# Attention and feed-forward kernel: inputs in tile order, row stacks by SBUF copies in place of DMA transposes

## The chip, the cores and the metric

The kernel runs on one core of one Trainium2 chip. The metric is the device time of one execution in microseconds; a lower time is better. Runs are repeated on the chip, and the median of the runs is quoted.

## The reference

Three layers follow one another; all of it is float32.

1. Causal attention with decay, 4 batches, 8 heads, 576 tokens, head dimension 64: `scores = q k^T / 8 + cum_t - cum_s`, where `cum` is the cumulative sum of `log(clip(f, 1e-4, 1))` per head; entries above the diagonal are masked; softmax over s; then times v.
2. A gated feed-forward layer with spatial mixing, on x of 4 x 576 x 512: `h = relu(x w_in)`; u and v are its two halves of 512 columns; v is normalised over its columns; `v_s[t] = sum_s w_spatial[t, s] v_n[s] + b_spatial[t]`; output `(u * v_s) w_out`.
3. A channel-mixing layer: `xk` and `xr` mix each token with the token before by `mu_k` and `mu_r`; `k = relu(xk w_k)`; output `sigmoid(xr w_r) * (k^2 w_v)`.

## The kernel before, in words

**Precision.** Products need more precision than one 16-bit pass gives. q and k are scaled by a power of two and split into a high and a low half-precision part. For each score tile two matmuls are added (L302): 128 rows that hold `k high` over `k low` against `q low` over `q high` (tiles kT and qT), and 67 rows that hold `k high` against `q high` with three rows for the cumulative sums (tiles kA and qA). The transposed scores (L335) are the same with 69 rows: the two further rows of qA carry the row maxima, high and low part.

**Work by pairs of heads.** A pair p is two heads, 16 pairs in all. `load` (L208 to L216) brings k and q of a pair with tokens on partitions, in rows of 64 values, into one of three buffers `knat`/`qnat`, by three DMAs each. `qksq` (L66) sums squares on ScalarE, `qkscale` (L78 to L250) makes the power of two on VectorE after a matmul with ones (L71), `qkhi` (L260 on ScalarE for k, L262 on VectorE for q) writes the high parts and `qklo` (L270 on VectorE) the low parts into `nk` or `nq`, side by side; a DMA transpose of 128 x 1280 half-precision values (L272) turns them into kT or qT. `kaux` (L278, L279) and `qaux` (L284) copy one half of kT and qT into kA and qA and load the rows of sums from the DRAM tile `cumd`; `crow` (L288, GpSimd) writes the constant rows of qA. Then come the scores (L302), the row maxima (L311, VectorE), and `mrow`: the maxima are split (L318, L319), turned by a matmul (L321), copied out (L323), written to the DRAM tile `md` (L325) and read back into two rows of qA (L326). `scoreT` (L335, then the exponential, L339), the causal mask (L344, GpSimd), the product with v (L357), the copy out of PSUM (L365), and per pair the reciprocals of the row sums, which go through DRAM (`head`, `recip`: L368, L375, L378, L381), and the normalisation (L388, GpSimd).

**v** is loaded per batch in five blocks of 128 tokens, two DMAs each (L222); between the two heads of a pair stand 64 columns of ones, which a memset writes once (L178), so that the product with v gives row sums too.

**The feed-forward layer** runs between the attention work of later pairs: `w_in` is loaded and converted from eight blocks at the start (L90, L97, L100 to L105, L440, L441), v half (L504), normalisation (L512 to L547), u half (L558, L560), spatial mixing (L575, L578) with the transposed weights `wspT`. `weights_spatial` (L444 to L485) loads w_spatial by rows, splits it block by block into high and low part, adds the bias in three half-precision columns (L473, L477), and transposes each block by DMA (L483).

**The last part** (L715) multiplies with w_out, w_k, w_r and w_v in single precision; its weights are converted on ScalarE and VectorE from about 395 us on, after the pool of the attention tiles is released; `mu` is loaded first there (L660).

**Order.** `plan_attention` and `plan_mlp` give each step a due time in units of one head and a priority (table `P`); `run` calls the steps in that order. The framework then orders each engine's instructions by its own model of time, except those that `pin` keeps in program order. Almost all DMAs are issued by SyncE (SP), whose queue runs in order: a DMA that waits holds up what is queued behind it. At the start ScalarE issues the first loads of q, f and one block of w_in.

## Time and profile before

| what | value |
|---|---|
| runs (3) | 752.95 to 754.21 us, median 753.43 us |
| profiled execution: span from first to last instruction | 750.9 us |
| profiled execution: its own time | the page gives none beyond the span; the runs shown lie 2.0 to 3.3 us above it |
| granted TensorE clock, mean | 0.970 |
| busy: PE, VectorE, ScalarE, GpSimd | 674.9, 426.8, 372.2, 184.5 us |
| DMA packets, bytes | 130681, 69.78 MB |

How to read the profile: PE is TensorE's matmuls and PEld its weight loads, which overlap them; DVE is VectorE, ACT ScalarE, POOL GpSimd, SP SyncE, and SPq, ACTq the queues of DMA issues of an engine. L272 is line 272 of the kernel. Busy time leaves out register, branch and semaphore instructions and DMA issues. A DMA share of 1 means that all 16 DMA engines are busy. `m<-xx,moe_w_k` means: tile m is written from tiles xx and moe_w_k. In brackets stands how long the engine was idle before an instruction, and what released it.

### The profile page before, as it was taken

Reading aid. Unit: us, or ns where it says so; the run is one execution under the profiler, and the core shown is the slowest. Engines: PE = TensorE matmul, PEld = TensorE weight load, DVE = VectorE, ACT = ScalarE, POOL = GpSimd, SP = SyncE. Lnnn points to the kernel's source line nnn. Section 1 sums busy time; section 2 is a strip of 40 time slices with the busy share of each in tenths; the row PEclk is TensorE's granted clock in tenths of the full one; section 3 lists DMA queues with packets and bytes.
Section 4 is the critical chain, followed back from the end, with each engine's and each line's share of the span. In section 5 each row is a group of like instructions: output and inputs, shape, how many; then the busy total and the mean of one; then the engine's idle time right before and its main releaser. Section 6 shows DMA issues by size and latency. Waiting matters only on the chain.

```text
span 750.9 us, 11016 instructions
## 1 busy us (share of the span) xinstructions
PE 674.9 (90%) x3718; PEld 499.5 (67%) x3718; DVE 426.8 (57%) x1147; ACT 372.2 (50%) x740; POOL 184.5 (25%) x385
## 2 busy tenths in 40 slices
PE   0377878989998999999997679999999999999997
PEld 0245545647775677666774458788888888888886
DVE  5987786666655656646026879988225512632342
ACT  4626786666426854355505539747225412622431
POOL 7122645555324544445321201000000000000000
PEclk9998968999999999999999899999999999999999
DMA  9997666765655234410025453450100100010010
GB/s 228 203 204 158 168 138 131 147 137 107 126 133 122 56 71 99 97 27 18 18 64 184 146 192 124 140 164 15 42 27 16 57 0 15 1 56 1 1 57 28
DMA packets 130681, 69.78 MB, mean 93 GB/s; under 512 B 114704, under 2 KB 115312, under 8 KB 130624
## 3 DMA queue, kind: packets, MB, share of 16 engines
q1 hardware_dynamic: 128032, 67.89, 37.1%
q10 hardware_dynamic: 2592, 1.19, 0.7%
q8 instruction: 29, 0.48, 0.3%
q14 instruction: 28, 0.23, 0.1%
HBM read 42.06 MB, written 9.79 MB: 69 GB/s over the span
## 4 chain that ended last, share of the span: by engine, by line
PE 60%; DMA 16%; DVE 10%; POOL 5%; issue 3%; ACT 3%; SPq 1%; DVEq 0%; ACTq 0%; POOLq 0%
PE m L715 40%; PE o L357 7%; DMA sr<-rd 3%; POOL x L388 3%; PE m L575 3%; PE m1v L504 3%; PE s L302 3%; PE t L335 2%; PE m1u L558 2%; DMA rd<-r 2%; DVE junk L311 2%; DMA r<-rd 2%; DMA wst<-in_moe_w_k_dram 1%; DMA rd<-xo 1%; DMA wst<-in_moe_w_in_dram 1%
## 5 line engine op out<-in xcount | busy, mean ns | idle before, releaser
L357 PE MATMUL o<-e,v 128*128 128x320 f32 (+4 forms) x448 | 114.0, 384 | 5.5 <-POOL e L344 3.7
L715 PE MATMUL m<-xx,moe_w_k 128*128 128x512 f32 (+1 forms) x480 | 107.5, 373 | 0.4 <-ACT x L710 0.4
L715 PE MATMUL m<-moe_w_v,k 128*128 128x512 f32 x432 | 104.8, 391 | 0.0
L339 ACT ACTIVATE e<-t,qa 128x512 f32<-128x512 f32 (+1 forms) x128 | 72.6, 590 | 50.4 <-PE t L335 50.1
L311 DVE CUSTOM_DVE_ANT_0 junk<-s,mask 128x512 bf16<-128x512 f32 (+4 forms) x160 | 75.9, 474 | 37.8 <-PE s L302 32.2
L715 PEld LDWEIGHTS m<-xx,moe_w_k 128*128 128x128 f32 x480 | 84.0, 188 | 18.1 <-ACT x L710 0.9
L357 PEld LDWEIGHTS o<-e,v 128*128 128x128 f32 x448 | 78.5, 199 | 23.7 <-POOL e L344 6.1
L715 PEld LDWEIGHTS m<-moe_w_v,k 128*128 128x128 f32 x432 | 80.7, 188 | 17.7
L344 POOL TENSOR_SCALAR_AFFINE_SELECT e<-e 128x128 f32<-128x128 f32 (+1 forms) x160 | 52.2, 342 | 125.5 <-ACT e L339 123.0
L751 DVE TENSOR_TENSOR tmp<-tmp 128x512 f32<-128x512 f32 (+1 forms) x40 | 25.5, 638 | 88.1 <-ACT tmp L750 87.9
L302 PE MATMUL s<-kT,qT 128*128 128x512 f16 (+2 forms) x192 | 55.8, 299 | 21.6 <-DVE nm L311 13.7
L504 PE MATMUL m1v<-win,xt 128*128 128x512 f16 x240 | 61.5, 397 | 0.0
L388 POOL TENSOR_TENSOR x<-xo,sr 64x576 f32<-64x576 f32 x32 | 47.0, 1469 | 47.6 <-DMA sr<-rd 46.4
L715 PE MATMUL m<-gh,moe_w_out 128*128 128x512 f32 (+1 forms) x240 | 55.1, 380 | 3.5 <-DVE u L578 3.5
L335 PE MATMUL t<-qA,kA 69*128 69x512 f16 (+2 forms) x192 | 51.6, 294 | 7.3 <-DMA qA<-md 6.7
L558 PE MATMUL m1u<-xt,win 128*128 128x288 f16 x384 | 53.6, 286 | 4.5 <-ACT u L560 4.5
L750 ACT ACTIVATE tmp<-m 128x512 f32<-128x512 f32 (+1 forms) x40 | 22.1, 556 | 71.6 <-PE m L715 71.4
L575 PE MATMUL m<-wspT,vn 128*128 128x288 f16 x384 | 54.4, 290 | 3.0 <-DVE u L578 2.3
L302 PE MATMUL s<-kA,qA 67*128 67x512 f16 (+2 forms) x192 | 50.6, 300 | 4.0 <-DMA kA<-kT 3.7
L701 POOL COPY x<-x 128x4 f32<-128x4 f32 x4 | 3.5, 884 | 198.1 <-ACT x L710 198.1
L715 PEld LDWEIGHTS m<-gh,moe_w_out 128*128 128x128 f32 x240 | 43.3, 193 | 13.0 <-DVE u L578 3.8
L335 PE MATMUL t<-qT,kT 128*128 128x512 f16 (+2 forms) x192 | 51.4, 293 | 0.0
(159 smaller groups left out, 1083.8 us busy)
## 6 DMA issues: line engine op xcount, KB each, us to landing
sr<-rd SPq DMA_DIRECT2D x32, 144.0 KB
gd<-u SPq DMA_DIRECT2D x16, 288.0 KB
out_dram<-o SPq DMA_DIRECT2D x18, 256.0 KB
knat<-in_k_dram SPq DMA_DIRECT2D x32, 128.0 KB
v<-in_v_dram SPq DMA_DIRECT2D x32, 128.0 KB
g<-gd SPq DMA_DIRECT2D x16, 256.0 KB
wst<-in_moe_w_k_dram SPq DMA_DIRECT2D x8, 512.0 KB
wst<-in_moe_w_v_dram SPq DMA_DIRECT2D x8, 512.0 KB
```

Source lines behind the costliest of these rows:

```text
L302: self.nc.tensor.matmul(s[:, o:o + n], self.tok(qn, p, h, 128 * ib - 64, 128)[0:r], self.tok(kn, p, h, k0, n)[0:r], start=(j == 0), stop=( ...
L311: self.nc.vector.tensor_tensor_reduce(out=self.junk[r0:, 0:n], in0=self.s[u % 2][r0:, o:o + n], in1=self.mask[r0:, m0:m0 + n], op0=ALU.add ...
L335: self.nc.tensor.matmul(t[:, o:o + n], self.tok(kn, p, h, 128 * c, 128)[0:r], self.tok(qn, p, h, q0, n)[0:r], start=(j == 0), stop=(j == 1))
L339: self.nc.scalar.activation(self.e[g][:, 512 * u:512 * u + n], t[:, 0:n], AF.Exp, scale=self.qa[p][:, 5:6])
L344: self.nc.gpsimd.affine_select(out=e, in_=e, pattern=[[1, n]], compare_op=ALU.is_ge, fill=0.0, base=0, channel_multiplier=-1)
L357: self.nc.tensor.matmul(o[:, 256 + f:256 + q1], v[:, c, h // 2, 64 * (h % 2):64 * (h % 2) + 128], e[:, off:off + q1 - f], start=(c == 0), ...
L388: self.nc.gpsimd.tensor_tensor(self.xp[r], self.xo[h][r], self.sr[r], ALU.mult)
L504: nc.tensor.matmul(self.m1p, xt[:, xs, 128 * j:128 * j + 128], self.win[:, ws, kc, 512:1024], start=(kc == 0 and n == 0), stop=(kc == 3 an ...
L558: self.nc.tensor.matmul(o, self.win[:, ws, kc, fs], self.xt[(4 * b + kc) % 8][:, xs, ts_], start=(kc == 0 and n == 0), stop=(kc == 3 and n ...
L575: nc.tensor.matmul(o, pairs[n][0], pairs[n][1], start=(n == 0), stop=(n == 13))
L715: self.nc.tensor.matmul(out, l, r, start=(first and j == 0), stop=(last and j == len(pairs) - 1))
L751: nc.vector.tensor_tensor(tmp[:, 0:n], tmp[:, 0:n], tmp[:, 0:n], ALU.mult)
```

## The change

The host hands q and k over as [16 pairs, 128, 576], two heads of 64 dimensions on the partitions and tokens along the row; v in blocks of 128 tokens with the ones and the zeros already between and behind the heads; w_spatial transposed, with its last 64 rows repeated; b_spatial as one row; mu in rows of four. In the kernel, one DMA loads k or q of a pair into one of two buffers `kraw`/`qraw`, the high and low parts are tiles of 128 x 576 of their own (two buffers each), and `stack` copies, for each head and each of k and q, three blocks of 64 rows by DMA from SBUF to SBUF: two into kT or qT and one into kA or qA. For the first pair the copies of q are issued by ScalarE. The loads are due 0.1 later. The rows of maxima go from SBUF into qA directly. The spatial weights are split in place into `wspT` without a transpose; the bias is split in one row of 576, held on three partitions, and its three parts are copied by DMA into three rows of `wspT`. `init` clears the columns of each tile that no stack writes.

```diff
-        self.nat = {(nm, i): at.tile([128, 2, 5, 64], F32, name=f"{nm}nat{i}") for nm in "kq" for i in range(3)}
+        self.raw = {(nm, i): at.tile([128, S], F32, name=f"{nm}raw{i}") for nm in "kq" for i in range(2)}
...
     def load(self, p, nm, q=None):
-        q = q or self.nc.sync
-        b, h0 = p // 4, 2 * (p % 4)
-        t, src = self.nat[nm, p % 3], self.a[nm]
-        for h in range(2):
-            q.dma_start(t[:, h, 1:5], src[b, h0 + h, 64:self.S].rearrange("(c p) d -> p c d", p=128))
-        q.dma_start(t[64:128, :, 0], src[b, h0:h0 + 2, 0:64].rearrange("h p d -> p h d"))
+        (q or self.nc.sync).dma_start(self.raw[nm, p % 2], self.a[nm][p])
 
     def vload(self, b, c):
-        t, src = self.v[b % 2], self.a["v"][b]
-        t0, tn = KB[c]
-        for e in range(2):
-            self.nc.sync.dma_start(t[:tn, c, :, 128 * e:128 * e + 64], src[e::2, t0:t0 + tn].rearrange("h p d -> p h d"))
+        self.nc.sync.dma_start(self.v[b % 2][:, c].rearrange("p a d -> p (a d)"), self.a["v"][b, :, c])
...
     def qkhi(self, p, nm, eng):
-        src = self.nat[nm, p % 3].rearrange("p h c d -> p (h c) d")
-        t = self.n16["n" + nm].rearrange("p h c d -> p (h c) d")
-        s = self.qa[p][:, 2 + n:3 + n]
-        hi = t[:, :, 64 * n:64 * n + 64]
+        hi = self.hi[nm] = self.at.tile([128, self.S], F16, tag="hi" + nm, bufs=2, name="hi" + nm)
+        src, s = self.raw[nm, p % 2], self.qa[p][:, 2 + n:3 + n]
...
     def qklo(self, p, nm):
-        nc.vector.scalar_tensor_tensor(t[:, :, 64 - 64 * n:128 - 64 * n], src, s, t[:, :, 64 * n:64 * n + 64], ALU.mult, ALU.subtract)
-        T = self.T[nm + "T", p % 3]
-        nc.sync.dma_start_transpose(out=T[:, 0:10], in_=t.rearrange("p c d -> p (c d)"))
+        hi = self.hi[nm]
+        lo = self.lo[nm] = self.at.tile([128, self.S], F16, tag="lo" + nm, bufs=2, name="lo" + nm)
+        nc.vector.scalar_tensor_tensor(lo, self.raw[nm, p % 2], self.qa[p][:, 2 + n:3 + n], hi, ALU.mult, ALU.subtract)
+
+    def row(self, nm, p, r0, r1, h):
+        return self.T[nm, p % 3].rearrange("p c t -> p (c t)")[r0:r1, 640 * h + 64:640 * h + 64 + self.S]
+
+    def stack(self, p, nm, h, q=None):
+        q = q or self.nc.sync
+        hi, lo = self.hi[nm][64 * h:64 * h + 64], self.lo[nm][64 * h:64 * h + 64]
+        up, down = (hi, lo) if nm == "k" else (lo, hi)
+        q.dma_start(self.row(nm + "T", p, 0, 64, h), up)
+        q.dma_start(self.row(nm + "T", p, 64, 128, h), down)
+        q.dma_start(self.row(nm + "A", p, 0, 64, h), hi)
 
     def kaux(self, p):
-        nc.sync.dma_start(t[0:64, 0:10], self.T["kT", p % 3][0:64, 0:10])
...
-    def qaux(self, p):
-        nc.sync.dma_start(self.T["qA", p % 3][0:64], self.T["qT", p % 3][64:128])
...
     def mrow(self, p):
-        d = self.hl.tile([2, 1280], F16, tag="md", bufs=2, name="md")
-        nc.sync.dma_start(d.rearrange("i (c t) -> (i c) t", t=128), r)
-        nc.sync.dma_start(self.T["qA", p % 3][67:69].rearrange("p c t -> p (c t)"), d)
+        for i in range(2):
+            nc.sync.dma_start(self.T["qA", p % 3][67 + i:68 + i], r[10 * i:10 * i + 10])
...
     def weights_spatial(self):
+        nc.sync.dma_start(ws, a["moe_w_spatial"].rearrange("c p t -> p c t"))
+        nc.sync.dma_start(wb, a["moe_b_spatial"].to_broadcast([3, S]))
...
-            for i in range(3):
-                x = nc.vector.tensor_copy(nf[:tn, 128 + i:129 + i], wbt)
...
-            self.pin(nc.scalar.mul(nf[:tn, 256:768], src[:, 0:512], s))
-            nc.scalar.mul(nf[:tn, 0:64], src[:, 512:S], s)
-            nc.scalar.mul(nf[:tn, 64:128], src[:, 512:S], s)
-            nc.vector.scalar_tensor_tensor(nf[:tn, 192:256], src[:, 512:S], s, nf[:tn, 0:64], ALU.mult, ALU.subtract)
-            nc.vector.scalar_tensor_tensor(nf[:tn, 768:1280], src[:, 0:512], s, nf[:tn, 256:768], ALU.mult, ALU.subtract)
-            nc.sync.dma_start_transpose(out=self.wspT[:, :, t0:t0 + tn], in_=nf[:tn])
+        pb = stp.tile([3, 3, S], F16, name="pb")
+        for i in range(3):
+            if i == 0:
+                self.pin(nc.vector.tensor_scalar(wb, wb, sw[0:3, 1:2], None, op0=ALU.mult))
+            nc.vector.tensor_copy(pb[:, i], wb)
+            if i < 2:
+                nc.vector.tensor_tensor(wb, wb, pb[:, i], ALU.subtract)
+        for i in range(3):
+            nc.sync.dma_start(self.wspT[i:i + 1, 1], pb[i:i + 1, i])
...
+            self.pin(nc.scalar.mul(hi, ws[:, c], s))
+            self.pin(nc.vector.scalar_tensor_tensor(lo, ws[r, c], s[r], hi[r], ALU.mult, ALU.subtract))
...
     def plan_attention(self):
-            add(T + P["aux"], 2, self.kaux, p)
-            add(T + P["aux"] + 0.1, 2, self.qaux, p)
+            for h in range(2):
+                add(T + P["aux"] + 0.2 * h, 2, self.stack, p, "k", h)
+                add(T + P["aux"] + 0.2 * h, 2, self.stack, p, "q", h, nc.scalar if p == 0 else None)
+            add(T + P["aux"], 3, self.kaux, p)
```

## Rows read from the trace of the kernel before

**Rows 1.** The page, parts 1 and 2: busy time of PE; DMA packets.
```profile
PE 674.9 (90%) x3718; PEld 499.5 (67%) x3718; DVE 426.8 (57%) x1147; ACT 372.2 (50%) x740; POOL 184.5 (25%) x385
...
DMA packets 130681, 69.78 MB, mean 93 GB/s; under 512 B 114704, under 2 KB 115312, under 8 KB 130624
```

**Rows 2.** Windows by stage; columns as the header line of the answer names them.
```profile
core 0: us, PE busy (x) PEld busy (x) DVE busy (x) ACT busy (x) POOL busy (x), PEclk, DMA share, GB/s
0.00:60.00 60.00, 26.36 (x122) 15.59 (x122) 47.37 (x139) 30.03 (x63) 24.59 (x63) 1.00 0.97 209
60.00:130.00 70.00, 57.19 (x297) 37.29 (x297) 51.63 (x200) 48.31 (x108) 31.25 (x57) 0.80 0.70 150
130.00:400.00 270.00, 260.66 (x1731) 178.34 (x1730) 140.59 (x469) 134.96 (x278) 117.27 (x238) 0.99 0.41 90
390.00:400.00 10.00, 10.00 (x68) 6.35 (x66) 3.54 (x10) 1.94 (x3) 2.04 (x2) 1.00 0.57 173
400.00:450.00 50.00, 34.04 (x221) 24.51 (x220) 38.76 (x73) 27.35 (x55) 7.90 (x25) 0.90 0.50 163
450.00:750.90 300.90, 296.66 (x1354) 243.75 (x1352) 148.49 (x269) 131.54 (x240) 3.54 (x4) 1.00 0.14 47
```

**Rows 3.** Timeline of the start, all engines: start us, duration us, engine, line.
```profile
9.14 0.72 ACT L66 ACTIVATE junka<-knat 128x640 bf16<-128x640 f32 x1
...
17.62 0.87 DVE L270 SCALAR_TENSOR_TENSOR nk<-knat,qa,nk 128x640 f16<-128x640 f32 x1
...
21.39 0.62 SPq L90 DMA_DIRECT2D wst<-in_moe_w_in_dram  x1
...
23.36 0.96 PE L302 MATMUL s<-kT,qT 128*128 128x512 f16 x2 [7.90 <-DMA kT<-nk]
...
28.01 0.96 PE L302 MATMUL s<-kA,qA 67*128 67x512 f16 x2 [3.69 <-DMA kA<-kT]
...
28.78 0.68 DVE L311 CUSTOM_DVE_ANT_0 junk<-s,mask 128x512 bf16<-128x512 f32 x1
```

**Rows 4.** Waits of PE: total us, times, longest.
```profile
PE s L302 <- DVE nm L311: 13.7, 16, 3.3
...
PE t L335 <- DMA qA<-md: 6.7, 5, 2.5
```

**Rows 5.** Timeline at 311 to 319 us: SP's queue and PE.
```profile
312.91 1.28 SPq L325 DMA_DIRECT2D md<-mr  x1
...
314.24 1.35 SPq L272 DMA_TRANSPOSE qT<-nq  x1
...
316.33 0.22 SPq L326 DMA_DIRECT2D qA<-md  x1
...
316.65 0.35 SPq L580 DMA_DIRECT2D gd<-u  x1
...
317.89 0.39 PE L335 MATMUL t<-qA,kA 69*128 69x512 f16 x1 [1.46 <-DMA qA<-md]
```

**Rows 6.** Issues of SP by tile (knat, then kT): ns min/median/max.
```profile
L215 SPq DMA_DIRECT2D knat<-in_k_dram x32: 368/504/1272, 0.8 to 235.7; - x32
...
L272 SPq DMA_TRANSPOSE kT<-nk x16: 1267/1393/1837, 19.7 to 311.5; - x16
L278 SPq DMA_DIRECT2D kA<-kT x16: 487/520/599, 23.4 to 317.1; - x16
```

**Rows 7.** The chain that ended last: start us, us, what.
```profile
115.63 3.67 DMA wspT<-n
...
318.73 1.83 DMA rd<-xo
```

**Rows 8.** Groups of instructions by line and shape, VectorE.
```profile
L270 DVE SCALAR_TENSOR_TENSOR nq<-qnat,qa,nq 128x640 f16<-128x640 f32 x16 | 16.3, 1016 | 0.1
...
L270 DVE SCALAR_TENSOR_TENSOR nk<-knat,qa,nk 128x640 f16<-128x640 f32 x16 | 14.8, 926 | 4.3 <-ACT nk L260 4.2
...
L262 DVE TENSOR_SCALAR nq<-qnat,qa 128x640 f16<-128x640 f32 x16 | 9.9, 622 | 1.0 <-DMA qT<-nq 0.9
```

More of the change, by code (lines that the diff above doesn't have):

```diff
@@ L141, in setup @@
         self.junka = at.tile([128, 640], BF16, name="junka")
-        self.n16 = {x: at.tile([128, 2, 5, 128], F16, name=x) for x in ("nk", "nq")}
         self.T = {(nm, i): at.tile([128, 11 if nm[0] == "k" else 10, 128], F16, name=f"{nm}{i}") for i in range(3) for nm in ("kT", "kA", "qT", "qA")}
@@ L163, in setup @@
         self.vp, self.vv, self.s = {}, {}, {}
+        self.hi, self.lo = {}, {}
     def init(self, i):
@@ L168, in init @@
         if i < 3:
-            for nm in ("kT", "kA"):
-                g.memset(self.T[nm, i][:, 10], 0.0)
-            t = self.T["kA", i].rearrange("p c t -> p (c t)")
-            g.memset(t[64:69, 0:1280], MS)
-            for h in range(2):
-                g.memset(t[64:69, 640 * h:640 * h + 64], 0.0)
-        elif i < 5:
-            t = self.v[i - 3]
-            x = g.memset(t[:, :, :, 64:128], 1.0)
-            if i == 4:
-                self.pin(x)
-            g.memset(t[64:128, 4], 0.0)
-        elif i == 5:
-            for nm in "kq":
-                g.memset(self.nat[nm, 2][0:64, :, 0, :], 0.0)
-        else:
+            g.memset(self.T["kA", i].rearrange("p c t -> p (c t)")[64:69, 0:1280], MS)
+            for nm in ("kA", "kT", "qT", "qA"):
+                t = self.T[nm, i]
+                if nm[0] == "k":
+                    g.memset(t[:, 10], 0.0)
+                g.memset(t[:, 0:10:5, 0:64], 0.0)
+        elif i > 5:
             self.pin(g.memset(self.xt[i - 6][:, :, 576:640], 0.0))
@@ L448, in weights_spatial @@
         ws = stp.tile([128, 5, S], F32, name="ws")
-        wb = stp.tile([128, 5, 1], F32, name="wb")
-        nc.gpsimd.memset(ws[64:128, 4, :], 0.0)
-        nc.gpsimd.memset(wb, 0.0)
-        nc.sync.dma_start(ws[:, 0:4], a["moe_w_spatial"][0:512].rearrange("(c p) s -> p c s", p=128))
-        nc.sync.dma_start(ws[0:64, 4], a["moe_w_spatial"][512:S])
-        nc.sync.dma_start(wb[:, 0:4], a["moe_b_spatial"][0:512].rearrange("(c p o) -> p c o", p=128, o=1))
-        nc.sync.dma_start(wb[0:64, 4], a["moe_b_spatial"][512:S, None])
+        wb = stp.tile([3, S], F32, name="wb")
+        nc.gpsimd.memset(am, 0.0)
+        nc.gpsimd.memset(self.wspT[0:64, 1], 0.0)
+        nc.sync.dma_start(ws, a["moe_w_spatial"].rearrange("c p t -> p c t"))
+        nc.sync.dma_start(wb, a["moe_b_spatial"].to_broadcast([3, S]))
         yield
@@ L611, in plan_attention @@
     def plan_attention(self):
-        add, G = self.add, self.B * self.H
+        nc, add, G = self.nc, self.add, self.B * self.H
         for p in range(G // 2):
@@ L857, with laid @@
     from concourse.bass_utils import run_bass_kernel_spmd as _run
+    def laid(name, x):
+        if name in "qk":
+            return x.transpose(0, 1, 3, 2).reshape(16, 128, 576)
+        if name == "v":
+            p = _np.zeros((4, 640, 4, 192), x.dtype)
+            p[:, 0:576, :, 64:128] = 1.0
+            p[:, 0:576, :, 0:64] = x[:, 0::2].transpose(0, 2, 1, 3)
+            p[:, 0:576, :, 128:192] = x[:, 1::2].transpose(0, 2, 1, 3)
+            return p.reshape(4, 5, 128, 768).transpose(0, 2, 1, 3)
+        if name == "moe_w_spatial":
+            t = x.T
+            return _np.concatenate([t, t[512:576]]).reshape(5, 128, 576)
+        if name == "moe_b_spatial":
+            return x[None]
+        if name in ("moe2_mu_k", "moe2_mu_r"):
+            return x.reshape(4, 128).T
+        return x
     nc = _bacc.Bacc("TRN2", target_bir_lowering=False, num_devices=1)
@@ L861 @@
     for name in _INS:
-        arr = _np.ascontiguousarray(inputs[name])
+        arr = _np.ascontiguousarray(laid(name, inputs[name]))
         if arr.dtype == _np.float64:
```

34 lines of the change are left out of this document (12 added, 22 removed).

## The prediction

> **What bounds the kernel now.** I read the page first, then the windows by stage, then the timeline of the start, then the waits of PE and the queue of SP. The page gives PE 674.9 us of a span of 750.9 us [rows 1], so 76 us are left in which PE has no matmul, and nothing in the change alters the number of PE's instructions in its long stages. What can be won is idle time and granted clock. The windows say where both lie [rows 2]: to 60 us PE is busy 26.4 of 60 us, from 60 to 130 us 57.2 of 70 us at a clock of 0.80, from 130 to 400 us 260.7 of 270 us, from 400 to 450 us 34.0 of 50 us, and after 450 us it is full. The share of DMA is 0.97 to 60 us, 0.70 to 130 us and 0.14 at the end. The change works in the first three stages; the last is bound by PE and only moves forward with its start.
>
> In the start [rows 3] the reader is to see two chains that meet. ACT sums the squares of the first k from 9.14 us. The last low part of the first pair ends at 18.49 us, its transposes are issued then, the first score matmul runs at 23.36 us, and its second half, which needs the copy into kA, at 28.01 us. Beside it, SP gets to the fourth block of the feed-forward weights only behind both transposes (21.39 us); VectorE converts that block before it takes the first row maximum at 28.78 us. VectorE is busy 47.4 of the first 60 us [rows 2] although the first k lands only at about 9 us: after that it is close to being the bound of the start itself.
>
> Later the waits of PE tell the rest [rows 4]: 13.7 us for row maxima, 6.7 us for the rows of maxima that reach qA by way of the DRAM tile md. At 312 us one sees how the second comes about [rows 5]: SP issues the write of md (1.28 us), a transpose (1.35 us), and only at 316.33 us the read of md into qA; PE then stood 1.46 us.
>
> **The change, part by part.**
>
> *Loads of q, k, v.* Per pair six issues become two, per batch ten for v become five. An issue for k takes 0.50 us (two of them) or, from the line of the first 64 tokens, about the same [rows 6], so some 3 us of SP per pair become 1 us. Packets under 512 B are 114704 of 130681 now [rows 1]; those of q, k and v, 256 B long, go. What that is worth: the DMA engines move 209 GB/s at a share of 0.97 in the first 60 us and 173 at 0.57, or 304 GB/s at a full share, where long weight rows are moved [rows 2]. The first k and q are 0.59 MB, at 304 GB/s 1.9 us; with 0.5 us for the issue [rows 6], the 1.8 us of a transfer of 2.2 KB (rd from xo, [rows 7]) and some waiting behind one another they land at about 5 us instead of 9 us. v now carries its zeros and ones, 1.97 MB per batch instead of 1.18 MB: the rest of DMA's time hides it (share 0.41 from 130 to 400 us), and without that cover it would cost 0.79 MB / 304 GB/s = 2.6 us per batch.
>
> *Transposes become stacks.* Per pair two transposes (1.4 us of SP each) and two copies (0.52 us each) go, 3.8 us [rows 6]; twelve copies of 64 rows come. No row shows such a copy; the nearest is the copy of 64 rows into kA, 0.52 us, and the lower bound is the 0.35 us of an issue with 128 long rows [rows 5]. Twelve are 4.2 to 6.2 us; I take 6 us. With the loads SP has per pair 3.0 + 3.8 = 6.8 us before and 1.0 + 6.0 = 7.0 us after. SP is not relieved, but its pieces are smaller. At the start half of the twelve go on ACT's queue: 3 us of issuing on an engine that is busy 30 of the first 60 us [rows 2], behind which only weight conversions and sums of squares wait.
>
> What the start gains: the bound above is the whole stretch from the last low part to the first full score, 28.01 - 18.49 = 9.5 us; below it is nothing, if VectorE's work decides and does not begin earlier. From the first landing to the first row maximum VectorE takes 28.8 - 9 = 19.8 us, nearly all of it work; begun 4 us earlier it is done at about 24.8 us. **I take 4.0 us** (0 to 9.5).
>
> *The detour through md.* From the issue of its write to that of its read SP shows 3.4 us at 312.91 us [rows 5]; the straight copies need no second wait. Of PE's 6.7 us **I take 5.0 us** (0 to 6.7); the row copies still queue behind others.
>
> *Shapes.* 640 columns become 576. The low parts take 1016 and 926 ns, the high part on VectorE 622 ns [rows 8]: a tenth of 2564 ns is 0.26 us per pair. ACT wins as little. VectorE limits PE in the first four pairs alone, so **1.0 us** (0 to 16 x 0.26 = 4.2).
>
> *Spatial weights.* Their five transposes go (one stands on the chain with 3.67 us, [rows 7]), with them two small ACT copies per block. On VectorE 25 operations on a single column become six on 576 columns of three rows, about 0.6 us each by the 622 ns above, so 3.6 us that are not surely less than what goes. **I take 1.0 us** (-1, if VectorE has more to do, to the 3.7 us of the chain).
>
> *mu.* Two loads of single words become loads of rows. They land before 400 us, where PE is busy 10.00 of 10 us [rows 2], so **nothing**; if that cover were gone, some of the 16 us in which PE idles from 400 to 450 us could come or go. Memsets that go or come on GpSimd: nothing, since GpSimd is busy 24.6 of the first 60 us and the conversions of the start do not pass through it.
>
> Sum: 4.0 + 5.0 + 1.0 + 1.0 = 11 us; 750.9 - 11 = 739.9 us of span. The three runs shown are 752.95 to 754.21 us, 2 to 3 us above the profiled span; with 2.5 us the forecast is **742.4 us**, 1.5% below the median.
>
> **Rivals.**
>
> *A, the start is VectorE's and the rest was hidden:* only some 4 us of waits go, 749 us. For it: VectorE at 47.4 of 60 us. Against it: its first work waits for a landing.
>
> *B, slower:* the twelve copies stand in SP's queue in one block between a pair's recip chain and its rows of maxima. The plan puts stacks and reciprocals at the same moment of the pair. Today a delay of 3.4 us on SP in front of the rows left PE idle for 1.46 us [rows 5]; a block of 6 us would leave it idle 2 to 2.5 us more, in 15 later pairs at 2 us some 30 us, less the 11 us won: 772 us. It decides when the block ends later than about 2 us after the cast of the maxima. Against it: the stacks are due 1.2 heads before their scores, some 12 us, so they can stand elsewhere. The Trainium skill (DMA: Bandwidth & Descriptors, Anatomy of one DMA) gives a transfer a fixed cost of about 2 us that is mostly the wait for completion; by that rule twelve transfers issued one behind the other pay it once, and B is weaker. The short transfer above agrees on the size, and no row here shows the overlap of twelve.
>
> *C, more:* the stage from 60 to 130 us has 12.8 us idle and a clock of 0.80 [rows 2]. If the stalls that go are those before which the clock fell, up to a fifth of 57.2 us, 11.4 us, is won too: 731 us. The Trainium skill (TensorE: Matmul & The Clock Gate, Part 1) says that an idle PE is set back to half clock, so that a stall costs more than its length; the windows from 60 to 130 us agree in kind.
>
> *D, no change:* the time saved comes back at 400 to 450 us, where ACT and VectorE convert weights, 752.5 us.
>
> **Chances.** Forecast (736 to 748 us) 0.52; C 0.20 and still lower 0.03; A 0.08; D 0.06; B 0.11. Range: the upper bounds are 9.5 + 6.7 + 4.2 + 3.7 = 24.1 us, 729 us, and half of C's clock below that, some 724 us; the high end is D with a little of B, 754 us. A measurement of this kernel tells 0.2% (1.5 us) from no change. Faster 0.83 (forecast, C, lower, A), same 0.06, slower 0.11.
>
> **What would show it.** Right: first full score near 22 us and first row maximum near 25 us; no wait of PE for md; a share of DMA clearly under 0.97 to 60 us; few packets under 512 B. Wrong: PE waiting for stacks or rows of maxima (B); first row maximum still at 28 us (A); PE idle for over 20 us from 400 to 450 us (D).

## The result, and the profile after

The changed kernel takes 760.81 us (760.02 to 761.82, 4 runs); the kernel before, on the same chip, 753.19 us (752.14 to 754.21, 4 runs). The ratio is 1.0107, with a 95% interval of 1.0083 to 1.0131: **slower by 1.1%**, where 1.5% faster was forecast. The profiled execution took 761.82 us with a span of 760.1 us, 9.2 us more than before.

The page and the waits of TensorE in the changed kernel, to be laid beside [rows 1] and [rows 4]; the columns of the waits are total us, times, longest:

```profile
PE 673.4 (89%) x3718; PEld 499.3 (66%) x3718; DVE 419.1 (55%) x1122; ACT 368.4 (48%) x730; POOL 178.2 (23%) x376
...
DMA packets 44464, 69.95 MB, mean 92 GB/s; under 512 B 11556, under 2 KB 24452, under 8 KB 44407
```
```profile
PE tot L71 <- ACT junka L66: 19.0, 2, 12.9
...
PE tot L71 <- ACT win L66: 7.3, 1, 7.3
PE o L339 <- POOL e L326: 6.8, 7, 2.7
...
PE t L317 <- DMA qA<-mr: 2.9, 3, 1.5
```

Everything that the change does directly is there. Short packets fell from 114704 to 11556; VectorE, ScalarE and GpSimd have less to do (419.1, 368.4 and 178.2 us against 426.8, 372.2 and 184.5); the wait for the rows of maxima fell from 6.7 to 2.9 us. And TensorE, with 1.5 us less to do, stands idle longer. The windows show in which stage, to be read against [rows 2]; the last three figures of a row are the granted clock of TensorE, the DMA share and GB/s:

```profile
0.00:60.00 60.00, 19.28 (x77) 10.97 (x78) 39.02 (x118) 24.03 (x52) 17.83 (x50) 1.00 0.78 234
60.00:130.00 70.00, 56.29 (x303) 36.78 (x301) 54.41 (x182) 46.55 (x100) 34.04 (x56) 0.84 0.41 114
130.00:400.00 270.00, 259.56 (x1730) 179.94 (x1729) 135.60 (x473) 137.14 (x282) 114.26 (x243) 0.99 0.33 89
```

To 60 us TensorE is busy 19.28 us instead of 26.36, 7.1 us less. VectorE, which was close to being the bound there, is now busy 39.02 of 60 us instead of 47.37: it too waits. DMA's share over the 60 us fell to 0.78 while its rate rose to 234 GB/s. That mean hides the beginning; from 4 to 28 us the DMA engines are busy throughout, as they are before (shares of 1.10 and 1.11 in the same three stretches):

```profile
4.00:12.00 8.00, 0.56 (x2) 0.50 (x2) 4.95 (x13) 4.78 (x10) 7.62 (x24) 1.00 1.01 357
12.00:20.00 8.00, 0.43 (x2) 0.43 (x2) 5.53 (x9) 0.78 (x2) 2.41 (x3) 1.00 1.04 387
20.00:28.00 8.00, 1.12 (x3) 0.28 (x3) 5.53 (x14) 5.70 (x15) 0.00 (x0) 1.00 1.02 267
```

So VectorE does not limit the start now, and up to 28 us the DMA engines are full. What they carry is another thing than before. The timeline of the first 36 us shows it (start us, duration us, engine, line):

```profile
4.42 8.36 SPq L204 DMA_DIRECT2D v<-in_v_dram  x9
4.42 0.68 ACT L66 ACTIVATE junka<-kraw 128x576 bf16<-128x576 f32 x1 [2.34 <-DMA kraw<-in_k_dram]
...
11.49 0.81 DVE L249 SCALAR_TENSOR_TENSOR loq<-qraw,qa,hiq 128x576 f16<-128x576 f32 x1
...
13.28 0.55 SPq L260 DMA_DIRECT2D kT<-hik  x1
...
14.24 0.52 ACTq L261 DMA_DIRECT2D qT<-hiq  x1
...
15.17 0.47 SPq L262 DMA_DIRECT2D kA<-hik  x1
...
16.18 0.47 ACTq L262 DMA_DIRECT2D qA<-hiq  x1
...
17.17 0.33 SPq L201 DMA_DIRECT2D kraw<-in_k_dram  x1
...
18.17 0.47 ACTq L260 DMA_DIRECT2D qT<-loq  x1
...
18.74 0.68 ACT L66 ACTIVATE junka<-qraw 128x576 bf16<-128x576 f32 x1 [6.92 <-DMA v<-in_v_dram]
...
19.57 0.59 PE L71 MATMUL tot<-qa,ones 128*128 128x2 f32 x2 [12.86 <-ACT junka L66]
...
25.00 0.96 PE L285 MATMUL s<-kT,qT 128*128 128x512 f16 x2 [4.84 <-DMA qT<-hiq]
...
33.14 1.31 SPq L267 DMA_DIRECT2D kA<-cumd  x2
...
35.42 0.95 PE L285 MATMUL s<-kA,qA 67*128 67x512 f16 x2 [0.70 <-DMA kA<-cumd]
```

The first k is there at 4.42 us, as forecast (9.14 us before, [rows 3]), and the low parts of the first pair are done at 12.3 us instead of 18.49. But SP issues nine loads of v in one stretch, which keeps its queue from 4.42 to 12.78 us; five of them are the first batch's, four the second batch's. The first stack copy stands behind them at 13.28 us. While the data of v move, each further issue comes some 2 us after the last, on SP (13.28, 15.17, 17.17 us) and on ScalarE's queue (14.24, 16.18, 18.17 us) alike, though it takes only half a microsecond itself. The two queues take turns: together they issue one transfer every 0.93 to 1.01 us, and a load of v of 384 KB takes 1.0 us at the 387 GB/s of that stretch. That the issues go at the pace at which the full DMA engines work off the loads in front is an estimate from these two numbers; no run tests it by itself. Behind those three copies of q on ScalarE stands the sum of squares of the second pair's q: ScalarE is idle for 6.92 us, the profile names a load of v as what ended it, and TensorE waits 12.86 us for the sum. The first half of a score starts at 25.00 us (23.36 before), and the second half, which needs the sums `cumd`, at 35.42 us (28.01 before): the write of `cumd` is issued at 23.71 us, its read into kA only at 33.14 us, behind fourteen other issues on SP.

How the delay travels is read from the timeline of TensorE. The first row is the start of the first full score, the next five that of the first transposed score with row maxima (L335 before) of a head, then the first matmul with `w_out`, then the span; all in us. The last three columns are kernels of the experiments below.

| | before | after | g1 | qg | ogs |
|---|---|---|---|---|---|
| first full score | 28.0 | 35.4 | 27.4 | 27.4 | 24.1 |
| head 1 | 47.4 | 53.9 | 45.6 | 47.6 | 45.0 |
| head 9 | 118.0 | 129.0 | 121.6 | 119.7 | 117.3 |
| head 17 | 205.4 | 212.6 | 205.0 | 207.6 | 199.1 |
| head 25 | 297.6 | 302.2 | 300.0 | 298.1 | 287.5 |
| head 32 | 367.0 | 374.1 | 372.3 | 366.2 | 355.9 |
| product with w_out | 444.9 | 452.8 | 450.1 | 443.4 | 432.4 |
| span | 750.9 | 760.1 | 756.1 | 750.2 | 738.9 |

The changed kernel is 7.4 us late at the first full score, 11.0 at head 9, 4.6 at head 25, 9.2 at the end. The delay of the start is the larger part, and the rest comes and goes in stages in which the change was to help.

### The profile page after: what moved, and what is told of

It reads as the page before. It is cut to its first block, busy times and chain, and to the rows that moved or that the text cites. A ratio compares the mean times of both kernels' runs of the same rounds, so it can differ in the third digit from the quotient of the medians.

```text
span 760.1 us, 11070 instructions
## 1 busy us (share of the span) xinstructions
PE 673.4 (89%) x3718; PEld 499.3 (66%) x3718; DVE 419.1 (55%) x1122; ACT 368.4 (48%) x730; POOL 178.2 (23%) x376
## 2 busy tenths in 40 slices
DMA packets 44464, 69.95 MB, mean 92 GB/s; under 512 B 11556, under 2 KB 24452, under 8 KB 44407
## 4 chain that ended last, share of the span: by engine, by line
PE 57%; DMA 16%; DVE 13%; POOL 5%; issue 4%; ACT 3%; SPq 2%; ACTq 0%; DVEq 0%; POOLq 0%
PE m L696 37%; PE o L339 7%; DMA sr<-rd 3%; PE m L554 3%; PE t L317 3%; PE m1u L537 3%; PE s L285 3%; DMA wst<-in_moe_w_k_dram 2%; DVE junk L294 2%; POOL x L370 2%; DMA rd<-r 2%; PE m1v L483 2%; DMA r<-rd 1%; DMA kraw<-in_k_dram 1%; DMA rd<-xo 1%
## 5 line engine op out<-in xcount | busy, mean ns | idle before, releaser
L326 POOL TENSOR_SCALAR_AFFINE_SELECT e<-e 128x128 f32<-128x128 f32 (+1 forms) x160 | 49.2, 325 | 126.1 <-ACT e L321 123.7
L554 PE MATMUL m<-wspT,vn 128*128 128x288 f16 x384 | 56.4, 294 | 5.3 <-DVE u L557 4.2
L483 PE MATMUL m1v<-win,xt 128*128 128x512 f16 x240 | 57.8, 379 | 0.0
L554 PEld LDWEIGHTS <-vn 128*128 128x128 f16 x384 | 38.1, 101 | 18.8 <-issue 6.0
```

The lines of the kernel that those rows point to most:

```text
L326: self.nc.gpsimd.affine_select(out=e, in_=e, pattern=[[1, n]], compare_op=ALU.is_ge, fill=0.0, base=0, channel_multiplier=-1)
L483: nc.tensor.matmul(self.m1p, xt[:, xs, 128 * j:128 * j + 128], self.win[:, ws, kc, 512:1024], start=(kc == 0 and n == 0), stop=(kc == 3 an ...
L554: nc.tensor.matmul(o, pairs[n][0], pairs[n][1], start=(n == 0), stop=(n == 13))
```

## The experiments

Three theories. **Theory 1:** the memset of ones into v, pinned in program order, held the loads of the second batch's v until it had run; with it gone, the planner (the framework's ordering of the engines) puts them into the start. **Theory 2:** the sums' rows stand behind the stack copies in SP's queue. **Theory O** (formed after the first runs): any edit makes the framework re-order all engines, and that alone costs some us.

### v's loads and the sums' queue

g1 puts one memset on GpSimd back into the changed kernel; c1 moves the write of `cumd` and its first three reads to ScalarE's queue; gc has both; x4 takes the kernel before and writes the rows of maxima straight to qA, and nothing else.

```diff
 g1
+        elif i == 4:
+            self.pin(g.memset(self.v[1][:, :, :, 64:128], 1.0))
 c1
-        nc.sync.dma_start(self.cumd.rearrange("i g c -> g i c"), kc)
+        nc.scalar.dma_start(self.cumd.rearrange("i g c -> g i c"), kc)
...
-        self.nc.sync.dma_start(t[64:67, 0:10]...
+        (self.nc.scalar if p < 3 else self.nc.sync).dma_start(t[64:67, 0:10]...
 x4
-        nc.sync.dma_start(d.rearrange("i (c t) -> (i c) t", t=128), r)
-        nc.sync.dma_start(self.T["qA", p % 3][67:69].rearrange("p c t -> p (c t)"), d)
+        for i in range(2):
+            nc.sync.dma_start(self.T["qA", p % 3][67 + i:68 + i], r[10 * i:10 * i + 10])
```

g1: 

> The changed kernel, with one memset put back: the columns of ones of the second v buffer are written again by GpSimd in program order, as in the kernel before, so that the loads of v for batch 1 (four of which SP now issues in the first 13 us, 1.6 MB) can't start before it. Theory 1 (those loads crowd the DMA rings: the second pair's q landed only at 18.7 us, ScalarE stood behind it for 6.9 us, and all else followed): that landing comes at 14 to 15 us, the first full score (the half with kA) moves from 35.4 to about 31 us, and the time falls by 3 to 5 us to about 756 us. Theory 2 (the start is late because the rows of sums for kA stand in SP's queue behind three pairs of stacks): first full score still within 1.5 us of 35.4 us, 759 to 761 us. Theory 3 (the loss of the start is caught up anyway, and the rest is later): score earlier, time unchanged.

c1: 

> The changed kernel, with the write of the cumulative sums to DRAM and their loads into kA for the first three pairs issued by ScalarE in place of SP; the v loads of batch 1 stay early. Theory 2 (order of SP's queue): the rows for kA land 5 us earlier or more, first full score at about 29 to 31 us, 755 to 757 us. Theory 1 (early v loads): the sums are moved, but ScalarE itself stands behind the late q of the second pair; first full score at 33 us or later, at most 2 us won, 758 to 761 us.

gc: 

> The changed kernel with both edits, gate on v and sums on ScalarE's queue. If theories 1 and 2 each hold a part, the gains add: first full score at 27 to 29 us, 752 to 754 us. If only one does, the time is that of the better of the two single runs. Theory 3: 759 to 761 us whatever the start does.

x4: 

> The kernel before with one part of the change alone: the rows of maxima go from SBUF into qA directly, without the DRAM tile md; transposes, loads and v as before. By the prediction's step PE's 6.7 us of waits for these rows shrink to under 2 us and the time falls by 3 to 6 us, to 747 to 750 us. Rival (PE has other work queued that only moves, or the rows still queue behind transposes): waits of PE for the rows still over 4 us, time 752 to 754 us.

Measured, with the kernel before at 754.18 us beside them: g1 756.71 us, ratio 1.0034 (1.0008 to 1.0060); c1 755.84 us, 1.0008 (0.9974 to 1.0042); gc 757.74 us, 1.0042 (1.0011 to 1.0073); x4 768.18 us, 1.0194 (1.0149 to 1.0240). The start of g1:

```profile
4.41 4.87 SPq L206 DMA_DIRECT2D v<-in_v_dram  x5
...
14.90 0.68 ACT L66 ACTIVATE junka<-qraw 128x576 bf16<-128x576 f32 x1 [3.34 <-DMA v<-in_v_dram]
...
20.82 0.96 PE L287 MATMUL s<-kT,qT 128*128 128x512 f16 x2 [4.50 <-DMA qA<-hiq]
```

Five loads instead of nine, ScalarE's wait 3.34 instead of 6.92 us, a DMA share of 0.82 instead of 1.02 from 20 to 28 us, the first full score at 27.4 instead of 35.4 us: the start is repaired, as theory 1 expected. The four loads that left it are 1.57 MB, some 4.1 us at 387 GB/s (an estimate), and the write of `cumd` comes 4.1 us earlier, the sum of squares 3.8 us. The rest of the 8.0 us goes with SP's order, which the edit changed too: the read of `cumd` follows its write by 4.9 us instead of 9.4, with seven other issues between them instead of fourteen.

Yet only 4.1 us of the time come back (760.81 to 756.71): g1 is 1.8 us ahead of the kernel before at head 1 and 5.3 us behind at head 32, for which no term of the prediction's sum accounts. And c1, with a first full score at 36.1 us, comes to 755.84 us all the same, where theory 1 expected 758 us or more. So with the planner free, 4 us of time cannot be put down to the start.

c1 does not decide on theory 2: the reads of `cumd` go on ScalarE's queue at 32.79 us, behind sums of squares, and so are late again. With the memset back the same move (gc) brings the first full score from 27.4 to 25.4 us; the sums' queue has a part in the start, and none that shows in the time (757.74 us, where 752 to 754 was expected if both theories hold a part).

Most telling is x4, which was to take only a wait away: it loses 1.9%, where both expectations lay between 747 and 754 us. TensorE's waits there:

```profile
PE t L334 <- ACT e L338: 8.6, 5, 2.5
...
PE o L356 <- POOL e L343: 7.6, 5, 3.4
```

The wait for the rows of maxima is gone from the head of the list, and waits for the exponentials (8.6 us) and for the causal mask (7.6 us, 3.7 before) have come up. The operations behind them were not touched.

### One part at a time, and one number

n1 changes one due time, no instruction. v1, w1 and s2 are the kernel before with one part of the change: v1 v's layout with its ones (and so without the memsets), w1 the spatial weights and mu, s2 q and k with the stacks and n1's due time (the rows of maxima still by way of md).

```diff
 n1
-P = dict(load=-8.0, ...
+P = dict(load=-7.9, ...
 v1
-            x = g.memset(t[:, :, :, 64:128], 1.0)
-            if i == 4:
-                self.pin(x)
...
-        for e in range(2):
-            self.nc.sync.dma_start(t[:tn, c, :, 128 * e:128 * e + 64], src[e::2, t0:t0 + tn].rearrange("h p d -> p h d"))
+        self.nc.sync.dma_start(self.v[b % 2][:, c].rearrange("p a d -> p (a d)"), self.a["v"][b, :, c])
```

n1: 

> The kernel before with one number changed: the due time of the loads of k and q is 0.1 of a head later (the change has this too). No instruction is added, removed or altered; only the order that the framework derives can differ. Theory O (much of what these variants differ by is the order in which the planner lays the instructions, not the cost of what was edited): the time moves by over 0.4%, 3 us, one way or the other, and PE's sums of idle time and of clock loss move with it. Rival (order is a detail, the edits themselves carry the difference): within 1.5 us of the kernel before.

v1: 

> The kernel before with the v part alone: blocks of v with their ones and zeros from the host, no memsets of v, one load per block. Theory 1 (without the memset the loads of batch 1 move into the start and crowd it): slower by 2 to 5 us, the first full score later than 28.0 us. Rival (v loads are hidden by other work, their issues are fewer): faster by 1 to 2 us, or the same.

w1: 

> The kernel before with the spatial weights and mu parts alone: no transposes of the spatial weights, bias as a row of 576. By the prediction's step 1 us faster (between 1 us slower and 4 us faster). Theory O: anything between 4 us faster and 8 us slower, with PE's waits in other places than at the spatial weights.

s2: 

> The kernel before with the q and k part alone: loads by head dimension, high and low parts of 128x576, twelve stack copies per pair in place of transposes; v, the detour through md, the spatial weights and mu as before. Theory 1 (the q and k part is good and the early v loads spoil it): faster than before by 2 to 6 us, first full score at 26 to 28 us. Rival B of the prediction (stacks in SP's queue hold up the rows of maxima and of sums): slower than before by 3 us or more, PE waiting for qA and kA rows by over 8 us in sum.

Measured, with the kernel before at 751.60 us: n1 755.95 us, 1.0059 (1.0029 to 1.0089); v1 762.62 us, 1.0145 (1.0100 to 1.0190); w1 758.38 us, 1.0087 (1.0051 to 1.0124); s2 751.31 us, 1.0003 (0.9976 to 1.0029). In n1 no instruction came, went or changed size, TensorE's matmuls stand in another order, and it loses 0.6%: that is theory O in its barest form, though what the later loads cost by themselves is not told apart from the order. The changed kernel has the same due time, so it has this edit too. v1 has the largest loss of the four, 11.0 us where theory 1 expected 2 to 5. Seven of its large loads are issued from 14.7 to 18.2 us, two of them the second batch's. Its start:

```profile
27.82 0.96 PE L292 MATMUL s<-kT,qT 128*128 128x512 f16 x2 [11.07 <-DMA kT<-nk]
```

Before, the same matmul waited 7.90 us and ran at 23.36 us [rows 3]. The time of s2 met neither expectation: it is that of the kernel before, and TensorE waits 8.2 us for the rows from md instead of 6.7. The three parts' ratios with that of x4 add up to some 4.3% of loss, against 1.1% for the whole change: these losses are not prices of the parts and cannot be summed.

### TensorE's order held

If the order is the cause, holding it must bring the gain out. First the matmuls were pinned in the order in which the plan calls them, the same in four kernels: pb (before), px (before without md), pa (after), pg (after with g1's memset).

```diff
-        self.nc.tensor.matmul(ps[:, 0:n], self.ones, col, start=True, stop=True)
+        self.pin(self.nc.tensor.matmul(ps[:, 0:n], self.ones, col, start=True, stop=True))
```
(and so for every matmul of the attention and feed-forward layers and of the last part)

pb: 

> The kernel before with every matmul held in the order in which the plan's due times emit it, so that PE's order no longer depends on the planner's model of time; this is the reference for the next three. Theory O expects that the order that the planner found for the kernel before was a lucky one: 755 to 775 us. Rival: within 3 us of the kernel before.

px: 

> As the run before, and the rows of maxima go straight into qA without the tile md; PE's order is the same, instruction by instruction. Theory O (md's removal is good, and the 14 us that it cost alone came from another order of PE): faster than the kernel before with PE's order fixed, by 2 to 6 us. Rival (the straight copies themselves are bad): slower than it by 5 us or more.

pa: 

> The changed kernel with PE's order fixed in the same way, the same order as the two runs before. Theory O with theory 1: the whole change gains 0 to 8 us against the kernel before with PE's order fixed, less what the early v loads cost at the start (4 to 7 us). Rival (the change costs by itself): slower than it by 5 us or more.

pg: 

> The changed kernel with the gate on the v loads of batch 1 and PE's order fixed in the same way. Theory 1: 3 to 7 us faster than the run before it, first full score near 27 us; with theory O it is the fastest of the four, 8 to 14 us under the kernel before with PE's order fixed, as the prediction's sum has it. Rival: within 2 us of the changed kernel with PE's order fixed.

Measured, with the kernel before at 752.54 us: pb 800.90 us, 1.0650 (1.0595 to 1.0706); px 793.18 us, 1.0551 (1.0500 to 1.0601); pa 790.29 us, 1.0509 (1.0458 to 1.0560); pg 781.80 us, 1.0386 (1.0333 to 1.0439). The plan's bare order costs the kernel before 48 us, since TensorE then stands before whatever is late:

```profile
PE t L335 <- DMA qA<-md: 30.4, 12, 7.4
```

That line is pb's; it was 6.7 us [rows 4]. But among four kernels with one order the change gains: without md 800.90 - 793.18 = 7.7 us, the whole change 10.6 us, with the memset back 19.1 us. With TensorE's order equal, the memset alone is worth 790.29 - 781.80 = 8.5 us, and the distance is there from the start: pg is 8.2 us ahead of pa at the first transposed score of head 1 (43.9 against 52.1 us) and 8.2 us at the end.

Then TensorE was given the order that the planner had found for the kernel before: qx (before without md), qa (after), qg (after with the memset), qs (s2).

```diff
+PE_ORDER = [(0, 3), (4, 1), (3, 1), (5, 24), (30, 6), ...
+    for x, y in zip(order, order[1:]):
+        tc.add_manual_dep(y, x.name, mybir.DependencyInfo(mybir.DependencyClass.NoSync, ...
```

qx: 

> The kernel before with the rows of maxima straight into qA, and every matmul held in exactly the place that it has in the kernel before. Theory O (md alone cost 14 us because the planner laid PE's work in another order): 746 to 752 us, PE's waits for the rows under 3 us. Rival (the straight copies cost by themselves): 757 us or more.

qa: 

> The changed kernel, whole, with every matmul in exactly the order of the kernel before; the early v loads remain. Theory O with theory 1: the start is still late by some 4 to 7 us, the rest gains what the prediction counted; 746 to 754 us against about 753 for the kernel before. Rival (the change costs by itself, whatever the order): 758 us or more.

qg: 

> The changed kernel with the gate on the v loads of batch 1, every matmul in exactly the order of the kernel before. Theory O with theory 1: the fastest so far, 738 to 747 us, 1 to 2% under the kernel before, first full score near 27 us and PE idle under 30 us up to 60 us. Rival: 753 us or more.

qs: 

> The q and k part alone (loads, 128x576 parts, stacks; md, v, spatial weights and mu as before), every matmul in exactly the order of the kernel before. Theory O: at or under the run of the q and k part in its own planned order (ratio 1.000 to the kernel before): 742 to 751 us. Rival B (stacks hold up other rows in SP's queue): 754 us or more, with PE waiting for qA from md by over 7 us.

Measured, with the kernel before at 751.59 us: qx 761.02 us, 1.0121 (1.0082 to 1.0160); qa 765.14 us, 1.0174 (1.0145 to 1.0204); qg 751.71 us, 1.0000 (0.9983 to 1.0016); qs 753.89 us, 1.0030 (1.0009 to 1.0052). The memset is now worth 765.14 - 751.71 = 13.4 us. Of these, 7.8 us are there at head 1 (47.6 against 55.4 us), nearly as much as in pg and pa; the rest comes later, while the other engines' order is still free. So theory 1 is firm for some 8 us of the start. But all four runs missed what theory O expected of them (746 to 752, 746 to 754, 738 to 747 and 742 to 751 us): the change as a whole gains nothing, and the shorter way of the maxima alone still loses, although TensorE waits only 0.5 us for the rows in qx. TensorE's order is not the whole. In qg one stall shows what is left, first on GpSimd, then on TensorE:

```profile
146.80 1.40 POOL L427 TENSOR_TENSOR x<-xo,sr 64x576 f32<-64x576 f32 x1 [6.34 <-DMA sr<-rd]
...
152.27 0.73 POOL L383 TENSOR_SCALAR_AFFINE_SELECT e<-e 128x128 f32<-128x128 f32 x3
```
```profile
152.62 2.39 PE L396 MATMUL o<-e,v 128*128 128x320 f32 x6 [5.48 <-POOL e L383]
```

GpSimd works through its queue in order. Here the normalisation, which waits for a transfer for 6.34 us, stands before the causal mask, and TensorE waits 5.48 us for the mask. In the kernel before the same queue is the other way round:

```profile
148.19 0.73 POOL L344 TENSOR_SCALAR_AFFINE_SELECT e<-e 128x128 f32<-128x128 f32 x3
152.30 1.40 POOL L388 TENSOR_TENSOR x<-xo,sr 64x576 f32<-64x576 f32 x1 [3.39 <-DMA sr<-rd]
```

TensorE does not wait for the 3.39 us there.

### All orders held

Two last kernels. ox is the kernel before without md, all engines and SP's queue in the order of before. ogs is the changed kernel with the memset back; the instructions that it shares with the kernel before stand in that kernel's order on TensorE, VectorE, ScalarE and GpSimd, as do the shared transfers of rows on SP, while loads and stacks are placed by the planner.

```diff
+ORDER = {"PE": "...", "DVE": "...", "Activation": "...", "Pool": "...", "SP": "..."}
+def fix_order(tc):
+    by = {i.name: i for i in tc.nc.cur_bb.bb.instructions}
+    for names in ORDER.values():
+        chain = [by["I-" + n] for n in names.split() if "I-" + n in by]
+        for x, y in zip(chain, chain[1:]):
+            tc.add_manual_dep(y, x.name, mybir.DependencyInfo(mybir.DependencyClass.NoSync, mybir.DependencyReason.DATA), reason="order")
```

ox: 

> The kernel before with the rows of maxima written straight to qA (no copy by DRAM), and with every instruction that is left in the same order as in the kernel before on all engines and on SP's queue, not on TensorE alone. With TensorE's order alone held, this edit measured 1.0121 (761 us). Theory O (that loss is the re-planned order of the other four engines): what is left is the gain of the shorter way, of which the waits at 66 and 102 us (2.7 and 2.1 us) are the measured part, so 746 to 751 us, a ratio of 0.992 to 0.998, and the row maxima's waits on TensorE below 4 us. Rival (the write straight to qA costs something itself, whatever the order): 757 us or more, a ratio of 1.007 or more.

ogs: 

> The changed kernel with one memset on GpSimd put back that holds the second batch's v loads, and with the instructions that it shares with the kernel before in the kernel before's order on TensorE, VectorE, ScalarE and GpSimd, and the shared row transfers on SP's queue too; the stack copies and the loads are placed by the planner. With TensorE's order alone held, it measured 1.0000 (751.7 us), with 5.6 us lost at 149 us behind GpSimd's queue. Theory O with theory 1 (order and v's gate are the whole loss): that loss goes, 738 to 749 us, a ratio of 0.98 to 0.996. Rival (the change has a price that no order takes away: the stack copies in SP's queue, or v's transfers): 752 us or more, a ratio of 1.000 or more.

Measured, with the kernel before at 753.08 us: ox 756.50 us (753.64 to 761.56), 1.0060 (1.0034 to 1.0086); **ogs 741.88 us (740.62 to 742.27), 0.9844 (0.9828 to 0.9860)**. ogs is 1.6% faster than the kernel before and 2.5% faster than the change by itself, and the fastest of all runs here. The theory of order and gate holds for the whole change. That holding all orders is no gain by itself is seen in ox; two controls were not run, the kernel before with its own orders held and the changed kernel without the memset under the same orders, so the memset's worth is measured with TensorE's order alone held.

ox lies between its two theories. Half of qx's loss is gone with the other engines' order. What is left has a place, as its wait list and its timeline at 58 to 69 us show:

```profile
PE t L352 <- DMA qA<-mr: 11.6, 7, 3.7
```
```profile
58.63 0.81 SPq L343 DMA_DIRECT2D qA<-mr  x1
62.88 2.15 SPq L290 DMA_TRANSPOSE kT<-nk  x1
65.08 0.83 SPq L343 DMA_DIRECT2D qA<-mr  x1
...
68.83 0.58 PE L352 MATMUL t<-qA,kA 69*128 69x512 f16 x1 [3.74 <-DMA qA<-mr]
```

The order of before gives the second row of maxima the old place of md's read, behind a transpose of 2.15 us, and a row written from SBUF into one partition costs SP 0.78 us of issuing (two per pair), where the write and the read of md had medians of 0.34 and 0.24 us:

```profile
L343 SPq DMA_DIRECT2D qA<-mr x32: 732/784/854, 44.1 to 359.3; - x32
```
```profile
L325 SPq DMA_DIRECT2D md<-mr x16: 273/342/1276, 43.6 to 355.2; - x16
L326 SPq DMA_DIRECT2D qA<-md x16: 222/242/833, 45.3 to 356.5; - x16
```

So the detour through DRAM is not itself the longer way: in that queue the rows wait 11.6 us instead of 6.7. Both expectations on ox missed: the edit has a price, 2 x 0.78 - 0.34 - 0.24 = 0.98 us of SP per pair, and the wait for the rows is short only where nothing long stands before the second one. In the changed kernel and in ogs the transposes are gone, and the wait is 2.9 and 2.7 us. No kernel was run that keeps md and has all other parts with every order held, so how much of ogs's gain this part carries stays open.

ogs by stage, and its largest waits:

```profile
0.00:60.00 60.00, 28.70 (x132) 17.60 (x133) 46.85 (x143) 30.80 (x69) 23.37 (x62) 1.00 0.76 233
60.00:130.00 70.00, 56.46 (x314) 37.58 (x314) 48.63 (x175) 47.09 (x98) 32.09 (x54) 0.85 0.47 130
130.00:400.00 270.00, 262.07 (x1754) 179.57 (x1753) 145.44 (x484) 138.92 (x292) 115.86 (x243) 0.99 0.34 98
400.00:450.00 50.00, 39.51 (x224) 29.74 (x223) 40.75 (x74) 29.01 (x55) 5.13 (x16) 0.90 0.48 152
```
```profile
PE tot L89 <- ACT junka L84: 12.7, 3, 9.2
...
PE o L359 <- POOL e L346: 3.7, 3, 2.8
...
PE t L337 <- DMA qA<-mr: 2.7, 2, 2.2
```

TensorE is busy 28.70 us in the first 60, against 26.36 before and 19.28 after, and VectorE is as busy as before (46.85 us). Of the three waits that grew in the changed kernel, that for the sum of squares of q (14.3 us before, 19.0 after) is 12.7, that for the sum of squares of w_in (`win`, 7.3 us after) is no longer in the list, and the mask is back at 3.7.

Where ogs wins its 12 us is not where the sum put them. By the table it is 3.9 us ahead of the kernel before at the first full score, 2.4 at head 1 and 0.7 at head 9, but 10.1 at head 25 and 12.0 at the end. From head 9 to head 25 the same 1116 matmuls in the same order take 170.2 instead of 179.6 us; the kernel before first, then ogs:

```profile
118.00:297.60 179.60, 169.99 (x1116) 116.56 (x1115) 107.04 (x364) 101.23 (x213) 84.42 (x168) 0.97 0.54 113
117.30:287.50 170.20, 165.85 (x1116) 114.94 (x1115) 101.33 (x357) 98.17 (x209) 82.82 (x165) 0.99 0.43 119
```

TensorE is idle 4.4 instead of 9.6 us there and busy 4.1 us less, at a mean granted clock of 0.99 instead of 0.97. In qg, with the other engines free, the stretch takes 178.4 us. Which part of the change brings the gain there was not tested.

## Why the prediction was wrong

The sign was wrong and the time lies above the range. Step by step:

**"v ... the rest of DMA's time hides it" and "Memsets that go or come on GpSimd: nothing": the step that failed.** The memset cost GpSimd nothing, as said, but its place in the order was a gate: v's second batch could not be loaded before it. What I weighed was how busy GpSimd is; what counted was who may start only after it. The size of v's larger blocks was weighed only from 130 us on, at a share of 0.41, although the loads of the first batch are issued in the start, where the share was 0.97 [rows 2]. At the start I had put half of the stacks on ScalarE's queue at "3 us of issuing", with "only weight conversions and sums of squares" behind them: it was the sum of squares behind them, late by 6.92 us of idle ScalarE, that held up the second pair. What the runs show in its place: the DMA engines are full from 4 to 28 us, and without the memset four loads of the second batch are among what they move first. Putting one memset back brought 8.5 and 13.4 us with TensorE's order held, some 8 us of it at the start; the 4.1 us with the planner free are inside what re-ordering does.

**The sum assumed that all else stays in its order.** That assumption stands in no line of the prediction; each term took a wait off the rows of before as if the others would stay. It is not so: one due time alone costs 0.6% (n1), and with all orders held and the gate back the same change gives 0.9844, where its like with TensorE's order alone gives 1.0000. Under these two conditions the sum of 11 us came close: ogs's span is 750.9 - 738.9 = 12.0 us shorter. That agreement is luck. The start and md were to bring 9 of the 11 us, and the kernel before waits 4.5 of its 6.7 us for md before head 9; yet ogs is only 0.7 us ahead there, and 9.4 us come from head 9 to head 25, where the kernel before waits 0.4 us for md and the sum had little else.

**The start, 4.0 us (0 to 9.5).** The landing came as forecast (4.42 us). In the changed kernel the first full score was 7.4 us later; in ogs it runs at 24.1 us, 3.9 us earlier, and the first row maximum at 26.7 against 28.8 us. An earlier landing does bring an earlier first row maximum, by 2.1 us with the gate and all orders, but 2.4 us are left at head 1 and 0.7 at head 9: as a term of the time, 4.0 us was too much.

**md, 5.0 us (0 to 6.7).** The wait fell by 6.7 - 2.9 = 3.8 us in the changed kernel. The reason given was wrong: not the second wait made the way long but the transposes ahead of it on SP, and the two straight writes cost SP more. Alone, with all orders held, the edit lost 0.6% (ox).

**Shapes, 0.26 us per pair.** Right: the three VectorE groups, beside [rows 8], sum to 2326 ns instead of 2564, 0.24 us less.

```profile
L249 DVE SCALAR_TENSOR_TENSOR loq<-qraw,qa,hiq 128x576 f16<-128x576 f32 x16 | 15.1, 946 | 0.0
L249 DVE SCALAR_TENSOR_TENSOR lok<-kraw,qa,hik 128x576 f16<-128x576 f32 x16 | 13.7, 858 | 1.4 <-ACT hik L240 1.2
L242 DVE TENSOR_SCALAR hiq<-qraw,qa 128x576 f16<-128x576 f32 x16 | 8.4, 522 | 0.1
```

**Spatial weights, 1.0 us (-1 to 3.7).** Not settled: with mu, in the planner's own order (w1), they measured 1.0087, no more than other small edits lost that way (n1 1.0059, x4 1.0194).

**The stacks.** The medians of their issues are 0.52 to 0.59 us, and twelve are some 6.8 us where 6 was taken (in the crowded start, 2 us apart).

**Rivals.** B named the right sign by another way: in the changed kernel the rows of maxima wait less, not longer. Where md is kept beside the stacks (s2 and qs), TensorE waits 8.2 and 9.0 us for the rows instead of 6.7, so B's mechanism is there in small; its price of 30 us never came. A fails: VectorE waits in the start. C expected the clock to rise with fewer stalls from 60 to 130 us; in ogs it is 0.85 against 0.80 although TensorE is idle 70 - 56.46 = 13.5 us there, against 12.8, so the link is not shown there. The clock did give something back elsewhere, from head 9 to head 25 in ogs, as told above. D expected the gain to come back as idle time at 400 to 450 us; in ogs TensorE is busy 39.5 of 50 us there, against 34.0, with part of the last stage already in that window. No rival named the order, though the kernel's description says that the framework orders each engine by its own model of time.

What stays open: why the planner's own order is worse for the changed kernel, which part of the change wins from head 9 to head 25, and whether an order made for it would beat ogs, whose order was made for the kernel before.

## What to carry to other kernels

Before an instruction is removed as free, ask what it held back: a memset, a wait or a pin can be the only thing that keeps a large load out of a crowded stretch. In a kernel whose engines are ordered by a planner, first measure what an edit that changes no instruction does to the time; losses below that size are no verdict on a part, and a part is judged with the order held. Hold the order on every engine that works through its queue in order, not on TensorE alone.

## What the runs showed of the hardware that was not expected

- Nine loads of v of 384 KB, 3.5 MB in all, kept SP's queue for 8.36 us at the start, although one issue takes only 0.33 to 0.53 us there: the rest are gaps between them, at a DMA share of 1.01 to 1.04 from 4 to 20 us. Until 19.5 us the issues on each of the two queues came only every 2 us, in turns. Whether the q copies would have gone through on SP's queue instead was not tried. One of the large loads stands on the chain that ended last with 6.95 us:

```profile
9.21 6.95 DMA v<-in_v_dram
```

- A row of maxima written from 10 partitions of SBUF into one costs SP 0.78 us of issuing, more than a stack copy of 64 rows (0.52 to 0.59 us) that moves 72 KB instead of 2.5 KB.
- The number of packets fell to a third, from 130681 to 44464, with nearly the same bytes (69.78 and 69.95 MB), and the kernel was slower all the same. The DMA share from 60 to 130 us fell from 0.70 to 0.41; what that is worth by itself was not measured.
